# The first two batches by pairs of heads instead of units of 256 tokens, in a retention and low-rank mixer kernel

## The chip, the cores and the metric

The kernel runs on one core of a Trainium2 chip. Five engines work from their own instruction queues: TensorE (PE in the profile, its weight loads PEld), VectorE (DVE), ScalarE (ACT), GpSimd (POOL) and SyncE (SP), which only issues transfers here. The metric is the device time of one execution in microseconds (us); less is better.

## The reference

Eight batches, eight heads, 576 tokens, head dimension 64. A retention layer (attention without softmax, with a decay per head) is followed by a low-rank token mixer and a two-layer channel MLP with a residual.

```python
scores = scale * np.matmul(q, k.transpose(0, 1, 3, 2))
gamma = 1.0 - 2.0 ** (-5.0 - np.arange(H))
Dmat = np.where(rel >= 0, gamma[:, None, None] ** rel[None], 0.0)   # rel = i - j
x = matmul(scores * Dmat, v)            # heads side by side: (8, 576, 512)
u = x + ((x.transpose(0, 2, 1) @ U) @ V).transpose(0, 2, 1)   # rank 32, over tokens
out = u + np.maximum(u @ w_ch1, 0.0) @ w_ch2                  # 512 -> 2048 -> 512
```

The inputs and the output are float32.

## The kernel before

The decay is split: `qscale` and `vscale` hold gamma to the power of plus and minus the position, so scores need only a triangular 0/1 mask. Within a batch the tokens are worked in blocks of 128. A block's output is its own masked scores times v (RV) plus q times a running state k^T v of all earlier blocks (QS); ST adds a block to the state.

A batch has 576 tokens, four and a half blocks, so two batches make nine blocks, and the fifth, index `J`, is shared: its lower 64 rows are batch 0's tail, its upper 64 rows batch 1's head. This is the half chunk (functions with `_J`).

After attention, x (tokens by 512) goes through the mixer: MA computes `a` = U^T x (rank 32 by 512), MH adds V^T a to x and gives u; u^T is needed as the input of the MLP. Y1 is the first layer, one step for each of 16 blocks of 128 hidden columns (`f`): four matmuls of 512 columns into a PSUM buffer of `ps_big` (three buffers), and one ScalarE ReLU copy (L482). Y2 (L511) is the second layer; VectorE adds u (L500) and POOL stores.

The order is written out by hand: each engine works its queue in program order. It has three parts.

- `startup` (L779): SyncE loads q, k, v of batches 0 and 1; batch 0's attention; then u^T of batch 0.
- `first_stretch` (L886): batch 1's attention, in between the Y1 steps of batch 0, which `y(n)` takes from a list; then u^T of batch 1 and the first Y1 steps of batch 1.
- `merge` (L16): the rest. Main work (Y1, Y2) of one pair of batches is mixed with the attention of the next by running cost, and with its loads and casts (`aux_items`). There, chunks of 128 tokens are transposed by the DMA queue (`xbar`, L259), and L275 is their score matmul. The chunks of batch 2 are numbered 9 and on.

In the first two parts, attention works on units of 256 tokens by all eight heads: units 0 and 1 are batch 0, 2 and 3 batch 1. A partition holds two neighbouring tokens, so one loaded piece has runs of 512 bytes. For each unit:

- `load_u` (L566): for each of k, q, v two transfers of 256 KB, four heads each, issued by SyncE.
- `cast_u` (L587): to bf16 on POOL (L592); `scale_u` (L594) multiplies v by its decay.
- `T_u` (L603): 16 TensorE transposes for k or for q into a PSUM tile, then one copy of 1024 columns to SBUF by VectorE (L620) or ScalarE (L618).
- `SC_u` (L626), 16 score matmuls of four heads into PSUM; `mask_u` (L641), one VectorE multiply of 1024 columns; twice a unit.
- `ST_u` (L684) and `Sblk` (L694): the state, copied to `sblk` by ScalarE.
- `RV_u` (L652), `QS_u` (L668), `XS_u` (L676): the output, scaled by VectorE to x.

So x of a batch is complete only after both units, and MA and u^T come after that. For batch 0, u^T is made directly in PSUM: transposing matmuls of x (L859) and then V^T a added on top (L874), copied by ScalarE and VectorE (L882, L884). For batch 1, MH makes u (L421, L427), which is transposed (L448) and copied (L452). `warm(n)` (L185) issues n matmuls without use, 128 by 512, that keep TensorE busy.

POOL also issues the weight transfers: `load_w1` (L194, four pieces) and `load_w2` (L200, eight pieces), which convert to bf16 on the way. SyncE's transfers use eight completion semaphores in turn.

Of the kernel before, what the change touches and what calls it, by code (L numbers as in the profile page):

```python
# [35 lines left out]
def kernel(  # L36
# [23 lines left out]
    J = 4  # L60
# [35 lines left out]
    vscaleU = consts.tile([P, 4, 2, H], FP32, name="vscaleU")  # L96
# [17 lines left out]
    def early_consts():  # L114
# [21 lines left out]
        nc.scalar.activation(out=vscaleU, in_=posU, func=AF.Exp, bias=lnb, scale=-1.0)  # L136
# [29 lines left out]
    def make_u():  # L166
        nc.scalar.activation(out=U_E[:, 0:J, :], in_=U_f[:, 0:J, :], func=AF.Copy)
        nc.scalar.activation(out=U_E[0:HALF, J, :], in_=U_f[0:HALF, J, :], func=AF.Copy)

        ps = ps_s.tile([P, 5, R], FP32, tag="pss", name="pu_o")  # L170
        nc.tensor.matmul(ps, swap, U_E, start=True, stop=True)
        nc.scalar.activation(out=U_O[0:HALF, 1:5, :], in_=ps[0:HALF, 0:4, :], func=AF.Copy)
        nc.scalar.activation(out=U_O[HALF:P, :, :], in_=ps[HALF:P, :, :], func=AF.Copy)
# [59 lines left out]
    def cast_qk(pr, i, rows=slice(0, P), eng=None):  # L233
# [4 lines left out]
        if eng is not None:  # L238
            for j in (1, 0):
                eng.tensor_copy(  # L240
                    out=t[rows, j, :], in_=c["f", j][rows].rearrange("p h d -> p (h d)"))
            return
# [222 lines left out]
    def y1_items(par, by_seg=False):  # L465
        nch = 4 + par
        segs = [(0, 4)] if par == 0 else [(0, 3), (3, 2)]
        items = []

        def Y1(f, seg):  # L470
            if f == 0 and seg == 0:
                st["y1", par] = y1_pool.tile(
                    [P, NF, nch * P], BF16, tag=f"y1{par}", name="y1")
# [86 lines left out]
    un = [dict() for _ in range(4)]  # L560
    st["x", 0] = x_pool.tile([P, NI, dm], BF16, tag="x", name="xt")

    def unit_i0(u):
        return 2 * u + (1 if u >= 2 else 0)

    def load_u(u, which):  # L566
        b = u // 2
        t0 = 2 * P * (u % 2) + HALF * b
        for j in which:
            dram = (q, k, v)[j]  # L570
            for hh in range(2):
                t = stage.tile([P, H, D], FP32, tag="stage", name="stage_t")
                un[u]["f", j, hh] = t
                nc.sync.dma_start(  # L574
                    out=t.rearrange("p (h j) d -> p h (j d)", j=2),
                    in_=dram[b, 4 * hh:4 * hh + 4, t0:t0 + 2 * P, :].rearrange(
                        "h (p j) d -> p h (j d)", j=2),
                )

    def unit_views(u, j, hh):  # L580
        if j not in un[u]:
            un[u][j] = qk_pool.tile([P, 2, dm], BF16, tag="qk", name="qk")
        w = slice(hh * 4 * D, (hh + 1) * 4 * D)
        return (un[u][j][:, :, w].rearrange("p j (h d) -> p h j d", d=D),
                un[u]["f", j, hh].rearrange("p (h j) d -> p h j d", j=2))

    def cast_u(u, j, hh, eng):  # L587
        o, f = unit_views(u, j, hh)
        if eng is nc.scalar:
            nc.scalar.activation(out=o, in_=f, func=AF.Copy)  # L590
        else:
            eng.tensor_copy(out=o, in_=f)  # L592

    def scale_u(u, hh, eng):  # L594
        o, f = unit_views(u, 2, hh)
        eng.tensor_tensor(
            out=o, in0=f,
            in1=vscaleU[:, u, :, 4 * hh:4 * hh + 4].rearrange("p j h -> p h j")[
                :, :, :, None].to_broadcast([P, 4, 2, D]),
# [3 lines left out]
    def T_u(u, j, eng):  # L603
        pst = ps_big.tile([P, 2 * NHP, P], BF16, tag="big", name="pst")
        for jj in range(2):
            for hp in range(NHP):
                nc.tensor.transpose(
                    pst[:, jj * NHP + hp, :], un[u][j][:, jj, hp * P:(hp + 1) * P], ident)
        t = qkT_pool.tile([P, 2 * NHP, P], BF16, tag="qkT", name="qkT")
        un[u]["T", j] = t  # L610
        o, i_ = t, pst
        if j == 0:

            o = t.rearrange("p a b -> p (a b)").rearrange(
                "p (hp t j) -> p j hp t", hp=NHP, j=2)
            i_ = pst.rearrange("p (j hp) t -> p j hp t", j=2)
        if eng is nc.scalar:
            nc.scalar.activation(out=o, in_=i_, func=AF.Copy)  # L618
        else:
            eng.tensor_copy(out=o, in_=i_)  # L620

    def qT(u):
        return un[u]["T", 0].rearrange("p a b -> p (a b)").rearrange(
            "p (hp t) -> p hp t", hp=NHP)

    def SC_u(u, hh, pool_, tag):  # L626
        psc = pool_.tile([P, 2, NHP, P], FP32, tag=tag, name="psc")
        kT, qt = un[u]["T", 1], qT(u)
        for hp in range(2):
            for jj in range(2):  # L630
                for s in range(2):
                    for hl in range(2):
                        r = slice(hl * HALF, (hl + 1) * HALF)
                        m = slice(s * HALF, (s + 1) * HALF)
                        nc.tensor.matmul(  # L635
                            psc[m, hl, hp * 2 + jj, :], kT[r, jj * NHP + 2 * hh + hp, m],
                            qt[r, 2 * hh + hp, s * P:(s + 1) * P], start=True, stop=True,
                        )
        un[u]["psc", hh] = psc

    def mask_u(u, hh):  # L641
        ret = ret_pool.tile([P, H, P], BF16, tag="ret", name="ret")
        nc.vector.tensor_tensor(  # L643
            out=ret.rearrange("p (a j) i -> p a (j i)", j=2),
            in0=un[u]["psc", hh].rearrange("p a b i -> p (a b i)").rearrange(
                "p (a ji) -> p a ji", a=4),
# [3 lines left out]
        un[u]["ret", hh] = ret  # L650

    def RV_u(u, hh):  # L652
        if "po" not in un[u]:
            un[u]["po"] = ps_o.tile([P, 2, dm], FP32, tag="po", name="po")
        for hp in range(2):
            for hl in range(2):
                h = 4 * hh + 2 * hp + hl
                for jj in range(2):
                    for s in range(2):
                        r = slice(s * HALF, (s + 1) * HALF)  # L660
                        nc.tensor.matmul(  # L661
                            un[u]["po"][:, s, h * D:(h + 1) * D],
                            un[u]["ret", hh][r, hl * 4 + hp * 2 + jj, :],
                            un[u][2][r, jj, h * D:(h + 1) * D],
                            start=(h == 0 and jj == 0), stop=True, skip_group_check=True,
                        )

    def QS_u(u, s, slot):  # L668
        for hp in range(NHP):
            nc.tensor.matmul(  # L670
                un[u]["po"][:, s, hp * P:(hp + 1) * P],
                qT(u)[:, hp, s * P:(s + 1) * P], sblk[:, slot, hp, :],
                start=False, stop=True, skip_group_check=True,
            )

    def XS_u(u, c0=0, c1=2):  # L676
        i0, n = unit_i0(u) + c0, c1 - c0
        nc.vector.tensor_tensor(  # L678
            out=st["x", 0][:, i0:i0 + n, :].rearrange("p s (h d) -> p s h d", d=D),
            in0=un[u]["po"][:, c0:c1, :].rearrange("p s (h d) -> p s h d", d=D),  # L680
            in1=qscale[:, i0:i0 + n, :, None].to_broadcast([P, n, H, D]), op=ALU.mult,
        )

    def ST_u(u, rows, acc, start):  # L684
        for hp in range(NHP):
            for jj in range(2):
                nc.tensor.matmul(  # L687
                    acc[:, hp, :], un[u][1][rows, jj, hp * P:(hp + 1) * P],
                    un[u][2][rows, jj, hp * P:(hp + 1) * P],
                    start=(start and hp == 0 and jj == 0), stop=True,  # L690
                    skip_group_check=True,
                )

    def Sblk(acc, slot):  # L694
        for hl in range(2):
            r = slice(hl * HALF, (hl + 1) * HALF)
            nc.scalar.activation(
                out=sblk[r, slot, :, hl * D:(hl + 1) * D],
                in_=acc[r, :, hl * D:(hl + 1) * D], func=AF.Copy)

    LO, HI, ALL = slice(0, HALF), slice(HALF, P), slice(0, P)

    def T_J(r):
        c = ch[0, J]
        pst = ps_big.tile([P, 2 * NHP, P], BF16, tag="big", name="pst")
        for j in range(2):
            for hp in range(NHP):
                nc.tensor.transpose(
                    pst[:, j * NHP + hp, r], c["qk"][r, j, hp * P:(hp + 1) * P],
                    ident[r, r])  # L710
        if "qkT" not in c:
            c["qkT"] = qkT_pool.tile([P, 2 * NHP, P], BF16, tag="qkT", name="qkT")
        nc.scalar.activation(out=c["qkT"][:, :, r], in_=pst[:, :, r], func=AF.Copy)

    def SC_J(r):
        c = ch[0, J]
        c["psc"] = ps_sc.tile([P, 2, NHP, P], FP32, tag="psc", name="psc")
        for hp in range(NHP):
            for hl in range(2):
                d = slice(hl * HALF, (hl + 1) * HALF)  # L720
                nc.tensor.matmul(
                    c["psc"][r, hl, hp, r], c["qkT"][d, NHP + hp, r], c["qkT"][d, hp, r],
# [3 lines left out]
    def mask_J(r):  # L726
        c = ch[0, J]
        if "ret" not in c:
            c["ret"] = ret_pool.tile([P, H, P], BF16, tag="ret", name="ret")
        nc.vector.tensor_tensor(  # L730
            out=c["ret"].rearrange("p (hp hl) i -> p hl hp i", hl=2)[r, :, :, r],
            in0=c["psc"][r, :, :, r],
            in1=tri[r, None, None, r].to_broadcast([HALF, 2, NHP, HALF]), op=ALU.mult,
        )

    def RV_J(r):
        c = ch[0, J]
# [276 lines left out]
```

## Time and profile before

| what | value |
|---|---|
| median of 3 runs | 337.58 us (336.85 to 338.22) |
| span of the profiled execution | 335.6 us |
| PE busy | 320.9 us, 96% |
| ACT, DVE, POOL busy | 139.2, 138.0, 78.2 us |
| chain that ended last, PE's share | 91% |
| of it Y1 (L477) and Y2 (L511) | 38% and 36% |
| Y1 step of 512 columns, one matmul | 0.33 us mean (with its end modelled) |
| POOL cast 128x512 (L592) | 0.61 us |
| mask 128x1024 (L643) | 1.22 us |
| k^T or q^T copy of 1024 columns | 0.69 us on VectorE (L620), 1.25 us on ScalarE (L618) |
| transfers | 36.85 MB read, 9.44 MB written |

The span runs from the first to the last instruction of the program; the device time has a little around it. "Chain" is the work that ended last, followed back step by step to whatever released it. Idle time of an engine off that chain costs nothing. In the views by stretch, each engine's busy time stands with its number of instructions, then the clock that TensorE was granted (1.00 is full), the busy share of the transfer engines and what they moved.

### The profile page before, as it was taken

What the parts mean: (1) busy time and instruction counts of PE and PEld (TensorE: products, weight loads), DVE (VectorE), ACT (ScalarE), POOL (GpSimd) and SP (SyncE); (2) the same over time, 40 slices, a digit from 0 to 9 for tenths busy, and PEclk for the clock granted to TensorE, in tenths of its full rate; (3) what the DMA queues carried; (4) which work ended last, traced back from release to release, by engine and by line L of the source; (5) the groups of instructions that cost most, each with busy time, mean ns of one, the idle gap of its engine ahead of it and who ended that gap; (6) DMA issues with size and microseconds to landing.
All of it is one profiled execution on the core that took longest, in us unless ns stands there. A gap on an engine that the chain in (4) does not pass through costs nothing.

```text
span 335.6 us, 6997 instructions
## 1 busy us (share of the span) xinstructions
PE 320.9 (96%) x2926; PEld 179.9 (54%) x2948; DVE 138.0 (41%) x190; ACT 139.2 (41%) x290; POOL 78.2 (23%) x112
## 2 busy tenths in 40 slices
PE   6688999899999999999999999999999999999996
PEld 3375554576544445446764455457754455457644
DVE  5453346433564234534356244524365144510022
ACT  2543665776210077107850176017740264037400
POOL 5686741211231140114102220222111100110000
PEclk9955999999999999999999999999999999999999
DMA  7999999999999929994998959995933400340012
GB/s 212 239 228 266 237 217 182 187 179 223 213 249 234 234 73 192 207 198 105 198 177 190 213 123 168 195 241 71 200 76 99 142 2 1 79 126 2 0 64 94
DMA packets 151311, 53.17 MB, mean 158 GB/s; under 512 B 131984, under 2 KB 148752, under 8 KB 151280
## 3 DMA queue, kind: packets, MB, share of 16 engines
q1 hardware_dynamic: 144512, 40.40, 64.7%
q0 software_dynamic: 6768, 12.32, 14.6%
q8 instruction: 23, 0.38, 0.5%
q14 instruction: 8, 0.07, 0.1%
HBM read 36.85 MB, written 9.44 MB: 138 GB/s over the span
## 4 chain that ended last, share of the span: by engine, by line
PE 91%; SPq 2%; issue 2%; DVE 2%; DMA 1%; ACT 1%; POOL 0%
PE ps_y L477 38%; PE ps_y L511 36%; PE psc L275 3%; PE po L314 2%; PE pss L687 2%; PE pss L340 2%; DMA stage_t<-in_q_dram 1%; SPq L574 1%; PE ph L421 1%; PE ps_y L522 1%; PE pa L394 1%; PE po L300 1%; PE po L661 1%; PE xT L859 1%; DVE xt L678 1%
## 5 line engine op out<-in xcount | busy, mean ns | idle before, releaser
L477 PE MATMUL ps_y<-uT,w_sb 128*128 128x256 bf16 (+2 forms) x768 | 137.0, 328 | 1.5 <-ACT uT L452 1.4
L482 ACT ACTIVATE y<-ps_y 128x384 bf16<-128x384 f32 (+2 forms) x192 | 90.0, 489 | 114.9 <-PE ps_y L477 114.2
L511 PE MATMUL ps_y<-w_sb,y 128*128 128x512 bf16 x538 | 124.3, 379 | 1.6 <-issue 0.8
L477 PEld LDWEIGHTS <-w_sb 128*128 128x128 bf16 x768 | 71.6, 98 | 46.7 <-issue 3.1
L511 PEld LDWEIGHTS <-y 128*128 128x128 bf16 x560 | 52.4, 98 | 60.3
L500 DVE TENSOR_TENSOR o_sb<-ps_y,u 128x512 f32<-128x512 f32 (+2 forms) x38 | 25.2, 663 | 76.6 <-PE ps_y L511 74.4
L503 POOL DMA_DIRECT2D out_dram<-o_sb x31 | 17.3, 558 | 158.6 <-DVE o_sb L500 152.8
L285 DVE TENSOR_TENSOR ret<-psc,tri 128x1024 bf16<-128x1024 f32 x24 | 29.4, 1225 | 47.3 <-PE psc L275 47.3
L254 POOL TENSOR_TENSOR vt<-stage_t,vscale 128x512 bf16<-128x512 f32 (+1 forms) x29 | 30.0, 1047 | 50.6 <-DMA stage_t<-in_v_dram 50.1
L325 DVE TENSOR_TENSOR xt<-po,qscale 128x512 bf16<-128x512 f32 x27 | 18.6, 691 | 25.9 <-PE po L314 25.9
L427 DVE TENSOR_TENSOR u<-ph,xt 128x768 bf16<-128x768 f32 (+2 forms) x24 | 21.8, 951 | 13.5 <-PE ph L421 13.5
L348 ACT ACTIVATE s_sb<-pss 128x512 bf16<-128x512 f32 x24 | 14.3, 597 | 8.3 <-PE pss L340 7.3
L245 ACT ACTIVATE qk<-stage_t 128x512 bf16<-128x512 f32 x27 | 16.5, 622 | 2.1 <-DVE o_sb L500 2.1
L243 DVE CAST qk<-stage_t 128x512 bf16<-128x512 f32 x27 | 16.3, 604 | 0.0
L400 ACT ACTIVATE a_sb<-pa 128x128 bf16<-128x128 f32 x8 | 2.2, 276 | 33.0 <-PE pa L394 33.0
L643 DVE TENSOR_TENSOR ret<-psc,triU 128x1024 bf16<-128x1024 f32 x8 | 9.7, 1222 | 11.3 <-PE psc L635 11.3
L314 PEld LDWEIGHTS <-ret 128*128 128x128 bf16 x216 | 10.0, 98 | 4.2
L592 POOL CAST qk<-stage_t 128x512 bf16<-128x512 f32 x16 | 9.6, 611 | 7.0 <-DMA stage_t<-in_q_dram 5.3
L275 PEld LDWEIGHTS <-qkT 64*128 64x128 bf16 x216 | 6.1, 94 | 9.1 <-issue 8.7
L275 PE MATMUL psc<-qkT 64*128 64x128 bf16 x216 | 10.7, 219 | 0.0
L314 PE MATMUL po<-vt,ret 128*128 128x64 bf16 x216 | 10.7, 193 | 0.0
L340 PE MATMUL pss<-vt,qk 128*128 128x128 bf16 (+1 forms) x96 | 9.3, 219 | 0.0
(103 smaller groups left out, 165.5 us busy)
## 6 DMA issues: line engine op xcount, KB each, us to landing
stage_t<-in_k_dram SPq DMA_DIRECT2D x32, 256.0 KB, 4.1
stage_t<-in_q_dram SPq DMA_DIRECT2D x32, 256.0 KB, 4.9
stage_t<-in_v_dram SPq DMA_DIRECT2D x32, 256.0 KB, 5.5
out_dram<-o_sb POOLq DMA_DIRECT2D x31, 256.0 KB, 3.8
w_sb<-in_moe_w_ch_dram POOLq DMA_DIRECT2D x4, 512.0 KB, 8.4
w_sb<-in_moe_w_ch_dram POOLq DMA_DIRECT2D x8, 256.0 KB, 10.2
stage_t<-in_k_dram SPq DMA_DIRECT2D x8, 128.0 KB, 4.2
stage_t<-in_q_dram SPq DMA_DIRECT2D x8, 128.0 KB, 4.0
```

The source lines that it names most:

```text
L245: nc.scalar.activation(out=t[rows, 0, :], in_=c["f", 0][rows].rearrange("p h d -> p (h d)"), func=AF.Copy)
L254: (eng or nc.gpsimd).tensor_tensor(out=c["v"][rows], in0=c["f", 2][rows], in1=vscale[rows, i, :, None].to_broadcast([n, H, D]), op=ALU.mult,)
L275: nc.tensor.matmul(psc[:, hl, hp, :], qkT[r, NHP + hp, :], qkT[r, hp, :], start=True, stop=True,)
L285: nc.vector.tensor_tensor(out=ret.rearrange("p (hp hl) i -> p hl hp i", hl=2), in0=c["psc"], in1=m[:, None, None, :].to_broadcast([P, 2, N ...
L314: nc.tensor.matmul(c["po"][:, hl, hp * D:(hp + 1) * D], c["ret"][:, h, :], c["v"][:, h, :], start=(first and hp == 0), stop=True, skip_gro ...
L325: nc.vector.tensor_tensor(out=xt[:, i, :].rearrange("p (hp hl d) -> p hl hp d", hl=2, d=D), in0=c["po"][:, :, 0:NHP * D].rearrange("p hl ( ...
L427: nc.vector.tensor_tensor(out=st["u", par][:, i0 - base:i0 - base + n, w].rearrange("p s (c d) -> p c s d", c=2), in0=ph[k][:, :, 0:n, :], ...
L477: nc.tensor.matmul(ps[:, 0:n, :], w1_sb[:, cc, f * P:(f + 1) * P], st["uT", par][:, c0:c0 + n, cc, :], start=(cc == 0), stop=(cc == NCC - 1),)
L482: nc.scalar.activation(out=st["y1", par][:, f, c0 * P:(c0 + n) * P], in_=ps[:, 0:n, :].rearrange("p s t -> p (s t)"), func=AF.Relu)
L500: nc.vector.tensor_tensor(out=o_sb[:, 0:n], in0=ps[:, 0:n], in1=st["u", par][:, c, w], op=ALU.add)
L503: (nc.sync if last else nc.gpsimd).dma_start(out=out_flat[r0:r0 + P, w], in_=o_sb[:, 0:n])
L511: nc.tensor.matmul(ps, st["y1", par][:, f, c * P:(c + 1) * P], w2_sb[:, f, :], start=(f == 0), stop=(f == NF - 1),)
```

## The change

Attention of batches 0 and 1 is worked by pairs of heads instead of units of tokens. One pair (`hp`, 0 to 3) covers all 512 tokens of a batch's four full blocks (for batch 0 the first 512, for batch 1 the last 512), and its two heads' 128 columns of x. MA and u^T need x by columns, so each pair can go from load to its own part of u^T.

- Loads: `load_h` issues, for each pair and each of k, q, v, two transfers of 128 KB (runs of 512 bytes as before). All of them, the half chunk's too, are in SyncE's queue, in the order in which they are used: pair 0, half chunk of batch 0, V, U, pairs 1 to 3, half chunk of batch 1, pairs 0 to 3 of batch 1. The constants are emitted after the loads.
- Half chunks: the two 64-row pieces are worked separately, both in the lower rows. Batch 0's outputs go to free columns of the pair's own PSUM tile (`RJ_h`, columns 256 to 383), scaled by `XSJ_h`.
- Each pair: `Tk_h`, `Tq_h` (four transposes each, into two parts of one PSUM tile), `SC_h`, `mask_h`, `ST_h`, `RQ_h` (RV and QS), `XS_h`, `XT_h` (transposing matmuls of x), `MA_h` (its 32 rows of a), `UT_h` (V^T a added, copies to u^T).
- Batch 1's u^T is made in the same way, the shared block by `UT_J`; `MH` of both batches moves behind the first Y1 steps of batch 1, and the transposes of u (L448) go.
- `make_u` is split; `dummy` matmuls like those of `warm` are put into the tiles that are about to be written.
- w1's pieces are issued by POOL between casts: piece 0 after pair 2, piece 1 in the half chunk of batch 1, pieces 2 and 3 in pairs 0 and 1 of batch 1.
- Six Y1 steps of batch 1, not three, are done before `merge`; the loads and casts of chunks 9 to 12 are emitted together before them.

```diff
-    def load_u(u, which):
-        b = u // 2
-        t0 = 2 * P * (u % 2) + HALF * b
...
+    def load_h(b, hp, j, eng):
+        t0 = HALF * b
+        t = stage.tile([P, H, D], FP32, tag="stage", name="stage_t")
+        sl[b][hp]["f", j] = t
+        for u in range(2):
+            eng.dma_start(
+                out=t.rearrange("p (u h j) d -> p u h (j d)", u=2, h=2)[:, u],
+                in_=(q, k, v)[j][
+                    b, 2 * hp:2 * hp + 2, t0 + 2 * u * P:t0 + 2 * (u + 1) * P, :].rearrange(
                         "h (p j) d -> p h (j d)", j=2),
...
+    def dummy(ap, n):
+        for _ in range(n):
+            nc.tensor.matmul(
+                ap, ident, ident[:, None, :].to_broadcast([P, 4, P]), start=True, stop=True,
+                skip_group_check=True)
+
+    def Tk_h(b, hp, ek):
+        c = sl[b][hp]
+        c["pst"] = ps_big.tile([P, 2 * NHP, P], BF16, tag="big", name="pst")
+        t = qkT_pool.tile([P, 2 * NHP, P], BF16, tag="qkT", name="qkT")
+        c["kT"], c["qT"] = t[:, 0:4, :], t[:, 4:8, :].rearrange("p a b -> p (a b)")
+        for u in range(2):
+            for jj in range(2):
+                nc.tensor.transpose(c["pst"][:, 2 * u + jj, :], c["qk"][:, 1, jj, u, :], ident)
+        copy(ek, c["kT"], c["pst"][:, 0:4, :])
...
+    def ST_h(b, hp, engs, n=0):
+        c = sl[b][hp]
+        acc_t = ps_s.tile([P, 4, P], FP32, tag="pss", name="acc")
+        dummy(acc_t, n)
...
+        def add(hl, n0, n1, lhsT, rhs):
+            nc.tensor.matmul(
+                acc[hl * HALF:(hl + 1) * HALF, n0:n1, :], lhsT,
+                rhs[:, None, :].to_broadcast([rhs.shape[0], n1 - n0, D]),
+                start=new[hl], stop=True, skip_group_check=True)
...
+    def startup():
...
+        def pool_h(hp):
+            cast_h(0, hp, 1, nc.gpsimd)
+            cast_h(0, hp, 0, nc.gpsimd)
+            scale_h(0, hp, nc.gpsimd)
+
+        A, V, G = nc.scalar, nc.vector, nc.gpsimd
+        warm(10)
+        pool_h(0)
+        cast_J(0, G)
+        scale_J(0, G)
+        pool_h(1)
+        pool_h(2)
+        load_w1(0)
...
+        SC_h(0, 2, 2)
+        mask_h(0, 2)
+        ST_h(0, 2, (A, A))
+        cast_h(0, 3, 1, A)
+        XT_h(0, 1)
+        MA_h(0, 1, A)
+        Tk_h(0, 3, V)
+        cast_h(0, 3, 0, V)
+        UT_h(0, 1, (A,))
+        Tq_h(0, 3, A)
+        scale_h(0, 3, G)
+        RQ_h(0, 2)
+        RJ_h(2)
+        XS_h(0, 2)
+        XSJ_h(2)
+        SC_h(0, 3, 2)
+        mask_h(0, 3)
+        ST_h(0, 3, (A, A))
+        XT_h(0, 2)
+        MA_h(0, 2, A)
+        UT_h(0, 2, (A,))
+        RQ_h(0, 3)
+        RJ_h(3)
+        XS_h(0, 3)
+        XSJ_h(3)
+        XT_h(0, 3)
+        warm(3)
+        MA_h(0, 3, A)
+        UT_h(0, 3, (A, V))
...
     def first_stretch():
...
+        for hp in range(NHP):
+            cast_h(1, hp, 1, G)
+            cast_h(1, hp, 0, G)
+            if hp < 2:
+                load_w1(hp + 2)
+            scale_h(1, hp, G)
+            T_h(1, hp, V, A)
+            if hp:
+                XT_h(1, hp - 1)
+                MA_h(1, hp - 1, V)
+            else:
+                RV_J(1, 0, H)
+                XS_J(1, 0, H)
             y(1)
+            SC_h(1, hp)
+            mask_h(1, hp)
+            ST_h(1, hp, (A, A))
+            y(1)
+            if hp:
+                UT_h(1, hp - 1, (V,))
+            y(1)
+            RQ_h(1, hp)
+            XS_h(1, hp)
         for f in range(0, NF, 2):
             load_w2(f)
+        XT_h(1, 3)
         y(1)
+        MA_h(1, 3, A)
+        UT_J(0, A)
         y(16)
+        UT_h(1, 3, (A, V))
+        UT_J(2, A)
+        aux = aux_items(NI, NI + 4)
+        for fn in aux:
             fn()
         Y1, rest = y1_items(1, by_seg=True)
...
+        for seg in (1, 0):
+            for f in range(2):
+                Y1(f, seg)
         MH0(outs0[0])
+        for fn in rest[2:4]:
+            fn[1]()
+        MH1(outs1[0])
+        for fn in rest[4:6]:
+            fn[1]()
+        MH1(outs1[1])
+        return rest[6:]
```

## The prediction

> **What bounds the kernel now.** I read the strips first, then the chain of waits in order of time, then stretches with the granted clock, then single groups in the first 66 us.
>
> ```profile
> PE   6688999899999999999999999999999999999996
> PEld 3375554576544445446764455457754455457644
> ...
> PEclk9955999999999999999999999999999999999999
> DMA  7999999999999929994998959995933400340012
> ```
>
> Each digit is a fortieth of the span, 8.4 us. TensorE is full from about 60 us to the end, so a change in the first two batches is worth what it moves TensorE's place in its own queue, no more. The clock strip has its only low digits at the start, and the DMA strip is full there too.
>
> ```profile
> 30.92 0.59 ACT uT L882
> ...
> 32.14 1.82 PE ps_y L477 x4
> ...
> 45.26 0.58 DVE xt L678
> 45.84 0.56 issue
> 46.40 0.69 DVE qkT L620
> 47.09 0.04 issue
> 47.13 1.02 PE ps_y L477 x4
> ...
> 61.18 1.46 PE ps_y L477 x8
> ...
> 64.20 3.64 PE ps_y L477 x28
> 67.84 0.33 PE psc L275 x8
> ```
>
> These are start, length and work along the chain. Batch 0's u^T is ready at 31.5 and its first Y1 begins at 32.1; batch 1's Y1 begins at 61.2; the first score matmul of batch 2 (L275) starts at 67.8, with five of batch 1's sixteen Y1 steps done. I compare the kernels at that last point. The three middle lines matter later: after RV, TensorE stood 1.9 us because VectorE did x first (L678) and only then the copy of the next k^T (L620).
>
> ```profile
> 7.60:11.00 3.40, 2.19 (x48) 1.51 (x48) 0.78 (x1) 1.55 (x2) 2.03 (x4) 1.00 1.14 254
> 11.00:14.40 3.40, 1.66 (x20) 0.76 (x12) 1.58 (x2) 2.09 (x2) 1.68 (x3) 1.00 1.21 225
> 14.40:17.80 3.40, 2.55 (x56) 1.64 (x57) 2.39 (x2) 1.87 (x4) 3.17 (x5) 1.00 1.32 223
> 17.80:21.20 3.40, 2.88 (x42) 2.49 (x43) 2.19 (x3) 1.51 (x4) 3.35 (x4) 0.50 1.13 173
> ...
> 31.50:34.90 3.40, 3.34 (x22) 1.42 (x22) 1.28 (x3) 1.69 (x4) 3.31 (x6) 0.50 1.20 243
> 34.90:38.30 3.40, 3.40 (x31) 1.97 (x30) 0.84 (x2) 2.33 (x5) 1.20 (x3) 1.00 1.22 268
> ```
>
> Busy us of PE, PEld, DVE, ACT and POOL, then the granted clock. Three stretches with TensorE busy 6.4 of 10.2 us, and the clock halves; it comes back after the first stretch of Y1 (2.8 us from 32.1).
>
> **The change, part by part.** I work out S, when batch 0's u^T is complete, then A, when batch 1's Y1 begins, then the first L275.
>
> *Loads.* 256 KB loads become twice as many of 128 KB. SyncE issues one per 0.54 us (0.74, 1.24, 1.78, 2.33 in the chain), the first landed 3.0 us after issue (first cast 3.77). 24 pieces and the 6 loads of half chunk, V and U: 0.74 + 30 x 0.54 + 3 = 19.9 for the last of batch 0. The bounds for the 24 extra issues are 0 (hidden behind the compute chain) and 24 x 0.54 = 13 us. I take 0: the third and fourth pairs' transposes come at 15.6 and 20.2 by the ledger below, and that pair's k and q are in by 18. If that cover goes, each late us is a us on S. A page rule bears on this: the Trainium skill, "DMA: Bandwidth & Descriptors", section "Rules for kernel authors", asks to coalesce many small transfers. No run here shows 128 KB pieces at the start; by its wish the loads would cost something, by the issue rows nothing.
>
> *Batch 0's chain.* Durations from the first 66 us: mask 1.22 (128x1024), POOL cast 0.61, scale 1.06, sblk copy 0.38, a_sb 0.27, q^T copy half of L618's 1.25 = 0.65, k^T copy half of L620's 0.69 plus start = 0.42, x in two halves 0.85 (L678: 1.22 for 1024; L755: 0.68 for 512), half chunk's x 0.3, uT 0.6. TensorE: 8 transposes 0.45 less their overlap = two of 0.25, SC 0.35, ST 0.5, RV+QS+half chunk 0.75, a dummy 0.22. The built program adds one wait the diff hides: the q transposes write the same PSUM tile as the k transposes and wait for VectorE's copy of k^T. In order: pair 0 casts to 5.8, k^T copy after the constants at 6.2, SC 7.5, mask 8.8, sblk 9.1, RQ 9.8; half chunk and V until 12; pair 1 SC 14.6, mask 15.8, RQ 17.3; pair 2 SC 18.1, mask 19.7, sblk 19.5. Pair 3's k cast is on ScalarE behind that (20.1), its q cast on VectorE (21.3), its q transposes 21.6, and pair 2's RQ stands behind them on TensorE: 22.4. Then x 23.25, half chunk 23.55, mask 24.8, RQ 25.9, x 27.05, XT, three dummies and MA 28.0, a_sb 28.3, UT 28.6, copies **S = 29.0**. Before: 31.5 to 32.1.
>
> *Batch 1 between Y1 of batch 0.* TensorE work from before's full-clock rows: a lone Y1 step 0.97 (32 to 61 us), 16 of them 15.5. Per pair: transposes 0.45, XT 4 x 0.069 = 0.28, MA 0.30, SC 0.35, ST 0.5, UT 0.22, RV 16 x 0.0215 and QS 4 x 0.069 = 0.62; together 2.72, four times 10.9. ST has no row (64-column weights, both halves of the output): 0.40 if the halves run side by side as SC's do, 0.65 if not; I take the middle. Half chunk: 0.35 + 0.35 + 0.37 + 0.1, and UT_J 12 x 0.056, 1.85. Sum 28.2. Before did this in 29.1 with 1.4 us lost to the half clock.
>
> *New waits there.* In each pair VectorE has x (0.85) and then the k^T copy (0.42) before the q transposes may go, while TensorE has only the k transposes (0.25): 1.05 idle, four times 4.2. Queued behind are XT, MA and a Y1 step. This is the 45.26 pattern, now once a pair. The half chunk's SC waits 0.35; the last XT waits for x 0.9; MA's copy stands behind a Y1 eviction, 0.65; the last copies 0.1. Sum 6.2, so **A = 29.0 + 28.2 + 6.2 = 63.4**, against 61.2.
>
> *After it.* The casts of chunks 9 and 10 now stand on ScalarE before Y1's evictions: 0.45 beyond three PSUM buffers. Chunk 10's q was cast at 61.0 before (0.62, not waiting), so it has landed. Before L275 there are now eight Y1 steps instead of five, 8 x 1.08 = 8.64, and the u of both batches (ph: 0.34 + 0.34 + 0.23 = 0.91), and 0.46 as between these pieces before: 73.9. Three Y1 steps less follow (3.24): 70.65 against 67.84, **2.8 us late with a full clock**. POOL's w1 and w2 issues are the same twelve at 0.74 to 0.84; w1's first piece goes at 17 and needs some 8 us, before S; nothing on the path. The memset, constants and allocations moved in the source cost nothing: their engines have them in the same place. The transposes by the DMA queue for chunk 9 were issued at 60.4 and have slack of 3 us before; A later gives them more.
>
> *Clock.* Changes lie 3.4 us apart in multiples (4.2, 17.8, 34.9). By my ledger TensorE has about 2.3, 2.9 and 2.9 us in the stretches up to 17.8 (23 dummies instead of 11, most of them early), then 1.9, 2.5 and 2.2 up to 28.1: 6.6 of 10.2, as before its loss. So I put the loss at 28.1, the regain at 34.9 as before: 0.5 on the tail of the chain, and 5.4 us of Y1 at half, 2.7: 3.2. Bounds: 0 (kept), and 4.65 (lost at 21.2: S 32.45 and 1.2 more). The Trainium skill, "TensorE: Matmul & The Clock Gate", section "Why this matters for your kernels", warns only of idle gaps over some 3 us; my ledger has none over 1.1, so by it the clock stays and the sum is the 2.8 alone. The trace lost it at 17.8 without such a gap (busy 2.55 of 3.4), and I follow the trace.
>
> The span is 335.6 and about 2 us lie around it, 337.6, which is the median of the runs shown (337.58). 337.6 + 2.8 + 3.2 = **343.6**.
>
> **Rivals.** *Clock kept*: 340.4. For it: more dummies; against: few after 18 us. *Pairs paced by their loads* (the other side): the hand-overs overlap better than my serial ledger, and S follows the last load of batch 0 at 19.9 by one chain (scale 1.06, ST 0.5, sblk 0.8, RQ 0.75, x 1.15, MA and UT 1.3) at 25.5; with UT pipelined 25. Price -4.0 with the clock kept: 336.4. It decides from S + idle below 32.4, where A falls under 61.2 in worth. For it: TensorE is busy only some 60% in my ledger; against: VectorE's x, copy, mask are in series there. Batch 1's waits halved as well would give 334.3; the casts before the evictions then hold Y1 at chunk 10's arrival (cast 61.0 before), so little below that. *Loads the bound*: each 128 KB as slow as a 256 KB step (0.95 us between casts) brings batch 0 in by 3.8 + 29 x 0.95 = 31, S 37: 350. Against: the DMA rate in the strip is already full. *It doesn't do what it says*: u^T of batch 0 no earlier than 32; that is the early loss of clock, 345.
>
> **How the numbers follow.** A clock loss, 343.6 to 345: 0.43. Clock kept, 340.4: 0.17. Loads: 0.03. These are the slower ones, 0.63. Load-paced: 0.37, of which 0.17 ends within 0.5% (1.7 us, about what a measurement of this kernel can tell) and 0.20 faster. The range reaches from 336.0, which leaves the faster ones out, to 347; the slower cases alone have 339 to 347.
>
> **What would show it.** S right: uT's copies of batch 0 end near 29. Waits right: VectorE's k^T copies in batch 1 follow x directly, and TensorE idles 1 us before the q transposes of each pair. Clock right: 0.50 in stretches between 28 and 35. Wrong: Y1 begins near 25, or TensorE is full from 25 to 60. First L275 near 74 to 77 is my sum; below 71 the change is a gain.

## The result and the profile after

The changed kernel takes 348.87 us (median of 4 runs, 346.52 to 350.8) against 337.29 us (336.85 to 338.22) for the kernel before: a ratio of 1.032, with a 95% interval from 1.027 to 1.037. It is slower, as forecast, by 11.6 us instead of 6.0, and above the range. The profiled execution took 350.8 us, with a span of 349.0, the longest of the four.

The page's strips of the changed kernel, a fortieth of the span (8.7 us) for each digit:

```profile
PE   8878888899999999999999999999999999999996
PEld 3444354456644444545775445446764445457644
...
PEclk9895599999999999999999999999999999999999
DMA  6799989739999996999499888896874400070012
```

TensorE looks busier in the first slices than before (8878 against 6688), and yet everything is later: 23 dummy products instead of 11 (beside the first ten of both) count as busy, and so does the longer time of products at half clock (three dummies 1.29 us instead of 0.65). A busy digit at the start is no progress. From the ninth slice on the PE strip is the same as before.

The chain of waits of the changed kernel in order of time (start, length, work), at the places that were shown of the kernel before:

```profile
36.68 0.60 PE xT L864
37.28 1.82 PE ps_y L483 x4
...
48.13 0.76 DVE xt L726 x2
48.88 0.34 DVE qkT L589
...
49.27 0.38 PE pst L632 x4
...
74.19 1.14 ACT qk L250 x2
75.33 0.28 ACT y L488
...
75.66 0.81 PE ps_y L483 x4
...
84.43 0.33 PE psc L280 x8
```

Batch 0's first Y1 begins at 37.3 (32.1 before; the forecast had u^T at 29.0), batch 1's at 73.9 (61.2), batch 2's first score product at 84.4 (67.8). With the three Y1 steps that are already done there, 84.43 - 3.24 - 67.84 = 13.35 us late. The spans differ by 349.0 - 335.6 = 13.4, so all of it is lost before 84 us: 5.1 in the start, 7.5 in the stretch from there to batch 1's Y1 (36.6 instead of 29.1), 0.7 after it. The middle lines are the forecast's wait: VectorE's x, then the copy of k^T, and TensorE idle until the q transposes.

The start of the changed kernel, in the same chain:

```profile
22.18 0.38 ACT sblk L587
...
22.58 0.64 ACT qk L587
...
23.27 0.41 PE pst L625 x4
...
24.05 0.79 DVE qk L589
...
24.88 0.40 PE pst L632 x4
25.27 0.54 PE po L710 x16
...
29.93 0.70 PE pa L843 x5
```

ScalarE copies pair 2's state (sblk), then casts pair 3's k; TensorE waits for it with the k transposes, then VectorE casts pair 3's q, and pair 2's RQ stands behind all this on TensorE until 25.3 (forecast: 21.6). It isn't the loads: pair 3's k landed at 18.44 and its q at 19.34, the last of batch 0 at 20.46 (forecast 19.9).

Stretches of the changed kernel, laid along the changes of clock (busy us of PE, PEld, DVE, ACT, POOL, then granted clock, share of the transfer engines, GB/s):

```profile
18.37:21.79 3.42, 2.90 (x65) 1.91 (x63) 1.79 (x5) 1.37 (x4) 2.44 (x4) 1.00 0.80 166
21.79:25.20 3.41, 1.75 (x18) 1.00 (x16) 1.88 (x3) 2.24 (x5) 1.68 (x3) 1.00 1.14 193
25.20:28.61 3.41, 3.41 (x54) 2.04 (x54) 1.23 (x4) 0.74 (x1) 1.14 (x2) 0.50 1.20 282
...
38.86:42.27 3.41, 3.41 (x26) 1.57 (x25) 0.28 (x1) 2.24 (x5) 2.27 (x3) 0.50 1.17 243
```

The stretch in which TensorE waits for those casts has 1.75 us of work in 3.41, and at its end the clock halves. It comes back at 42.3, after a stretch filled mostly by Y1: 17.1 us at half clock, most of them on the chain. An earlier drop, from 11.5 to 15.0 us, adds 3.4.

### The profile page after: what moved, and what is told of

It is laid out like the page before. It is cut to its first block, busy times and chain, and to the rows that moved or that the text cites. A ratio compares the mean times of both kernels' runs of the same rounds, so it can differ in the third digit from the quotient of the medians.

```text
span 349.0 us, 7266 instructions
## 1 busy us (share of the span) xinstructions
PE 335.4 (96%) x3024; PEld 182.3 (52%) x3024; DVE 142.5 (41%) x216; ACT 140.6 (40%) x302; POOL 77.9 (22%) x111
## 4 chain that ended last, share of the span: by engine, by line
PE 93%; DVE 2%; ACT 1%; DMA 1%; SPq 1%; issue 1%; POOL 0%; ACTq 0%
PE ps_y L483 37%; PE ps_y L517 35%; PE psc L280 3%; PE po L319 2%; PE pss L345 2%; PE ph L426 1%; DMA stage_t<-in_q_dram 1%; PE acc L677 1%; PE ps_y L528 1%; PE pa L843 1%; PE pw L195 1%; PE po L305 1%; DVE xt L726 1%; PE xT L864 1%; PE po L710 1%; SPq L578 1%
## 5 line engine op out<-in xcount | busy, mean ns | idle before, releaser
L517 PE MATMUL ps_y<-w_sb,y 128*128 128x512 bf16 x560 | 126.9, 380 | 0.0
L506 DVE TENSOR_TENSOR o_sb<-ps_y,u 128x512 f32<-128x512 f32 (+2 forms) x38 | 25.2, 663 | 73.2 <-PE ps_y L517 71.0
L290 DVE TENSOR_TENSOR ret<-psc,tri 128x1024 bf16<-128x1024 f32 x24 | 29.4, 1224 | 45.2 <-PE psc L280 45.2
L259 POOL TENSOR_TENSOR vt<-stage_t,vscale 128x512 bf16<-128x512 f32 x27 | 28.1, 1050 | 53.5 <-DMA stage_t<-in_v_dram 41.6
L432 DVE TENSOR_TENSOR u<-ph,xt 128x1024 bf16<-128x1024 f32 (+2 forms) x24 | 21.8, 952 | 13.6 <-PE ph L426 13.6
L589 POOL CAST qk<-stage_t 128x512 bf16<-128x512 f32 (+1 forms) x18 | 11.0, 610 | 13.0 <-DMA stage_t<-in_k_dram 8.1
L726 DVE TENSOR_TENSOR xt<-po,qscale 128x256 bf16<-128x256 f32 x16 | 6.1, 420 | 12.7 <-PE po L823 6.9
```

The costliest lines, as they stand in the source:

```text
L259: (eng or nc.gpsimd).tensor_tensor(out=c["v"][rows], in0=c["f", 2][rows], in1=vscale[rows, i, :, None].to_broadcast([n, H, D]), op=ALU.mult,)
L290: nc.vector.tensor_tensor(out=ret.rearrange("p (hp hl) i -> p hl hp i", hl=2), in0=c["psc"], in1=m[:, None, None, :].to_broadcast([P, 2, N ...
L432: nc.vector.tensor_tensor(out=st["u", par][:, i0 - base:i0 - base + n, w].rearrange("p s (c d) -> p c s d", c=2), in0=ph[k][:, :, 0:n, :], ...
L506: nc.vector.tensor_tensor(out=o_sb[:, 0:n], in0=ps[:, 0:n], in1=st["u", par][:, c, w], op=ALU.add)
L517: nc.tensor.matmul(ps, st["y1", par][:, f, c * P:(c + 1) * P], w2_sb[:, f, :], start=(f == 0), stop=(f == NF - 1),)
```

## The experiments

Theory: three terms add up. The start is late by its own chain (pair 3's casts, and the one PSUM buffer of `ps_s`); its idle time costs the clock; batch 1's pairs cost some 6 us in the stretch, half of it the wait for k^T. Rivals: one of the two batches is all of it; the clock falls whatever is done; the loads pace it. Every kernel's numbers stand here: when the record of batch 0's first Y1 product starts and how long it is from there to batch 1's, both from the profiled execution; the time; and the mean granted clock of its runs (0.01 is some 7 us at half clock).

| kernel | first Y1, us | to batch 1's Y1, us | median, us (range) | clock of the runs |
|---|---|---|---|---|
| before | 32.07 | 29.1 | 337.29 (336.85 to 338.22) | 0.974 (profiled) |
| changed | 37.21 | 36.6 | 348.87 (346.52 to 350.80) | 0.971, 0.975, 0.990, 0.989 |
| units_pairs | 27.97 | 35.1 | 341.19 (337.64 to 342.34) | 0.990, 0.985, 0.985, 1.000 |
| pairs_units | 36.72 | 32.0 | 344.39 (342.57 to 347.27) | 0.960, 0.975, 0.984, 0.975 |
| k_first | 36.70 | 36.1 | 349.71 (349.32 to 350.30) | 0.975, 0.971, 0.975, 0.975 |
| cast3_pool | 32.54 | 36.2 | 345.04 (344.01 to 346.25) | 0.990, 0.994, 1.000, 0.989 |
| c3_no_dummies | 34.02 | 35.9 | 347.38 (346.90 to 350.19) | 0.959, 0.951, 0.960, 0.960 |
| c3_pa_big | 30.25 | 35.3 | 342.72 (342.02 to 344.34) | 1.000, 1.000, 0.999, 1.000 |
| own_q_y | 36.27 | 33.4 | 343.64 (343.00 to 346.67) | 0.975, 0.989, 0.989, 0.985 |
| before_late_half | 25.84 | 30.0 | 336.31 (335.46 to 339.46) | 0.970 to 0.995 |
| filled | 32.16 | 35.3 | 345.22 (344.45 to 347.60) | 1.000, 1.000, 1.000, 0.985 |
| pa_big | 35.60 | 36.6 | 346.20 (345.08 to 349.20) | 0.975, 0.989, 0.984, 0.989 |
| c3_pa_own | 30.27 | 32.1 | 341.05 (339.61 to 344.44) | 0.999, 1.000, 0.995, 0.995 |
| units_own | 27.34 | 31.8 | 336.39 (334.66 to 339.00) | 0.990 to 1.000 |

The kernel before, run beside them, had medians of 336.87 (the first four), 335.92 (the next four) and 336.20 (the last four).

### Which batch: units_pairs and pairs_units

```diff
 units_pairs: startup() of the kernel before (half chunk's upper part and w1's second piece left
 to the stretch), then first_stretch() of the changed one
+        load_J(1, nc.sync)
+        for hp in range(NHP):
+            for j in (1, 0, 2):
+                load_h(1, hp, j, nc.sync)
 pairs_units: startup() of the changed kernel, then first_stretch() of the one before
+        load(0, J, (1, 0, 2), seg=1)
+        load_u(2, (1, 0, 2))
+        load_u(3, (1, 0, 2))
```

> Batch 0 as in the kernel before (units), batch 1 by pairs as in the changed one. Theory (the loss has two parts that add: batch 0's u^T is 5.2 us late, 37.3 against 32.1 us, and the stretch from there to batch 1's Y1 is 36.6 instead of 29.1 us): u^T back at 32, stretch about 35.5 (a little less of it at half clock), so batch 1's Y1 at 67.6 and some 342 to 343.5 us in all. Rival (the start is all of it, the stretch only long because it starts late and at half clock): first Y1 at 32, the stretch back near 30, 337 to 338.5 us.

> Batch 0 by pairs as in the changed kernel, batch 1 by units as before. Theory (two parts that add): u^T of batch 0 stays at 37 us, the stretch is 29 to 31 us, 342 to 344 us. Rival (the start is hidden, batch 1's stretch is all): 337 to 339 us. Rival (the half clock from 25 us is all): first Y1 at 37 and 344 us or more, with the clock low till 42.

Both halves cost. Batch 1 by pairs keeps its long stretch (35.1) even when it starts 9 us earlier; batch 0 by pairs keeps its late u^T (36.7) with batch 1 by units. The ratios to the kernel before are 1.014 (1.006 to 1.021) and 1.026 (1.019 to 1.033). So it is not one batch alone. The rival of the clock isn't excluded here: the signs that it named for pairs_units (first Y1 at 37, 344 us or more, a low clock until 42) all came, with a clock that was low until 41.7; filled, below, answers it. units_pairs was a little faster than the theory's sum: its first Y1 came at 28 instead of 32, with 6.8 us at half clock instead of 17.1. That the clock is the reason is not shown (before_late_half, below).

### The wait for k^T: k_first and own_q_y

```diff
 k_first: the next pair's k transposes and copy ahead of x; a Y1 step ahead of XT
             RQ_h(1, hp)
+            if hp + 1 < NHP:
+                head(hp + 1)
             XS_h(1, hp)
 own_q_y: q transposes in their own tiles; the same Y1 step ahead of XT
+            pq = ps_big.tile([P, 2 * NHP, P], BF16, tag="big", name="psq")
+            t = qkT_pool.tile([P, 2 * NHP, P], BF16, tag="qkT", name="qqT")
             T_h(1, hp, V, A)
+            y(1)
             if hp:
                 XT_h(1, hp - 1)
                 MA_h(1, hp - 1, V)
...
-            y(1)
             SC_h(1, hp)
```

> In batch 1 each pair's k transposes and the copy of k^T now stand before the previous pair's x on VectorE, and a Y1 step lies between the q transposes and the XT that needs x. Theory (TensorE's 1.15 us idle in three pairs is the wait for that copy behind x): 0.7 to 0.8 us less per pair, 2 to 2.5 us less in all, 346 to 347 us. Rival (the wait only moves to XT, which now waits for x): 0 to 0.5 us less, 348.5 us.

> Changed kernel; in batch 1 the q transposes get their own PSUM and SBUF tiles, so that they no longer wait for VectorE's copy of k^T, and a Y1 step stands between them and the XT that needs x. Theory (each pair's 1.15 us of TensorE idle is that wait): 0.9 to 1.1 us less per pair in three pairs, 0.4 in the first, batch 1's Y1 3 us earlier after the first Y1, 345.5 to 346 us. Rival (the stretch is bound elsewhere, by VectorE or by GpSimd's casts): less than 1 us, 348 us or more.

k_first moved the wait instead of removing it: TensorE still stood 0.5 us between the k and q transposes, and ST, with MA now shortly ahead of it, took 0.65 us in the chain instead of 0.46. A pair's period went from 6.87 to 6.54, and the time at the same clock (0.971 to 0.975) from 349.7 and 350.8 to between 349.3 and 350.3: nothing that can be told. own_q_y removes the shared tile. The chain of own_q_y:

```profile
46.89 0.22 PE pst L625 x4
47.12 0.22 PE psq L637 x4
47.34 0.86 PE ps_y L483 x4
48.20 0.25 PE xT L859 x4
```

k transposes, q transposes and Y1 now follow one another with no VectorE row between them, and a pair's period is 5.90: 0.97 less, what the theory said. The stretch is 3.2 us shorter. At a clock near 0.99 it takes 343.0 to 343.95 against 346.5 and 348.0, at 0.975 346.7 against 349.7: 3 us or somewhat more. The median lies 2 us below the expectation, with three of its four runs at the higher clock.

### Pair 3's casts, the PSUM buffer: cast3_pool, pa_big, c3_pa_big

```diff
 cast3_pool
         load_w1(0)
+        pool_h(3)
...
-        cast_h(0, 3, 1, A)
...
-        cast_h(0, 3, 0, V)
...
-        scale_h(0, 3, G)
 pa_big (and, on top of cast3_pool, c3_pa_big)
-        pa = ps_s.tile([P, P], FP32, tag="pss", name="pa")
+        pool_, tag = (ps_s, "pss") if b else (ps_big, "big")
+        pa = pool_.tile([P, P], FP32, tag=tag, name="pa")
```

> The casts and the scaling of batch 0's fourth pair go to GpSimd behind w1's first piece; ScalarE and VectorE lose theirs. Theory (pair 3's q transposes at 24.9 us, behind VectorE's cast, hold pair 2's RQ): pair 2's RQ starts near 23 instead of 25.3, first Y1 at 35 to 35.8 instead of 37.3, 1.5 to 2.3 us less, 347 us. Rival (another wait, such as the one PSUM buffer that MA, ST and the dummies share, ends at the same time): first Y1 within 0.5 us of 37.3, no change.

> Changed kernel; batch 0's MA in a PSUM buffer of the pool of three, and nothing else. Theory (this wait is a term by itself): MA01 no longer waits for the state's copies, but pair 3's k cast on ScalarE, behind those copies, still holds the k transposes until 23.2, so 0.3 to 1 us less at equal clock, 347 to 348.5 us. Rival (it and the casts add in full): first Y1 2 us earlier, 346 to 347 us.

> On top of cast3_pool: batch 0's MA writes a PSUM buffer of the pool of three instead of the single one that the state sums use too. Theory (MA01 and MA02 wait for both sblk copies, 0.85 us each, with k transposes, RQ and SC of the next pair queued behind): 1.2 to 1.8 us less, first Y1 at 31, 343.5 us. Rival (the k transposes then wait for a buffer of the three, or for the casts): within 0.5 us of cast3_pool.

cast3_pool brings the first Y1 4.7 us forward, twice what was expected, and most of that goes with the clock. In the changed kernel the first drop had already put pair 1's SC at 16.72; here it starts at 15.53. Of the 2.2 us by which pair 2's RQ starts earlier (23.1 against 25.3) that leaves 1.0 for the casts; the other 2.5 come later, where the clock now is full until 29.4. pa_big alone starts its first Y1 at 35.6 with the clock at half from 23.4 to 40.4, and its time is 2.7 us lower in the median, but 0.5 (349.2 against 349.7) and 1.1 to 1.4 (345.1 and 345.4 against 346.5) at like clocks, 0.975 and 0.989: nearer to the theory, though the clock's scatter is as large. On top of cast3_pool it gives 2.3 us at the first Y1, 30.25, and the clock stays full in all four runs. Pair 3's RQ, ahead of cast3_pool's drop at 29.4, starts at 26.44 instead of 27.46: 1.0 is the buffer, and the other 1.3 come where cast3_pool runs at half clock.

### The clock: c3_no_dummies and filled

```diff
 c3_no_dummies: cast3_pool without its dummy products after the first ten
-        warm(2)
...
-        SC_h(0, 1, 3)
+        SC_h(0, 1)
...
 filled: the changed kernel with eight more, in a tile of ps_big
+        fill(3)
         MA_h(0, 1, A)
+        fill(2)
         Tk_h(0, 3, V)
...
+        fill(3)
         MA_h(0, 2, A)
```

> On top of cast3_pool (first Y1 at 32.5 us, 345.0 us): the dummy products after the first ten are all left out (46 weight loads and products, 23 of each). Theory (the dummies stand on the chain: 4.8 us of them in its rows from 11.8 us on, some 2 us of which other waits would fill): first Y1 at 29.5 to 31, 342 to 343.5 us. Rival (without them the clock is lost earlier and for longer): first Y1 at 33 or later, half clock before 20 us, 346 us or more.

> Changed kernel with eight more dummy products where TensorE waits in batch 0's second half: three ahead of MA01 (it waits 0.85 us for the state's copies), two ahead of pair 3's k transposes (waiting for the cast on ScalarE, 0.6 us), three ahead of MA02. At full clock each takes 0.22 us, so all lie inside those waits. Theory (the clock falls at 25 us because TensorE was too idle before; the late half clock is 6 to 7 of the 11.6 us): clock kept to the first Y1, first Y1 near 33 to 34, 344 to 346 us. Rival (the clock falls whatever TensorE does there, or the dummies only lengthen the chain): first Y1 at 37 to 38, 348 to 350 us.

Without dummies the rival was right: the clock halves at 9.8 us, after a stretch of 3.4 us in which TensorE was busy for 1.69, and stays so for 27.3 us; 347.38 against 345.04. With eight more of them, nothing else changed, the clock is full in three of four runs and the first Y1 starts at 32.2 instead of 37.2. Stretches of filled, laid as those of the changed kernel:

```profile
18.91:22.32 3.41, 3.41 (x53) 1.95 (x53) 2.13 (x4) 1.66 (x4) 1.78 (x3) 1.00 0.87 133
22.32:25.73 3.41, 2.88 (x60) 1.64 (x57) 1.68 (x6) 1.34 (x2) 0.00 (x0) 1.00 1.20 221
25.73:29.15 3.42, 3.06 (x47) 1.79 (x43) 1.21 (x2) 1.62 (x4) 2.85 (x4) 1.00 1.09 244
```

The same casts, the same loads and the same waits, but 2.88 us busy where the changed kernel had 1.75, and no drop. So filled is the changed kernel at full clock, and splits its loss: the clock is 350.8 - 344.45 = 6.35 us in the profiled executions, and 348.87 - 345.22 = 3.65 in the medians, since two runs of the changed kernel had a clock of 0.99 without any filling; the rest is not the clock. Nor is all of the 6.35 the work of the eight products. The first of them comes at 20.6, and the drop at 11.5 is missing in filled as well, with the same queue of TensorE up to there: its stretch before that place lies from 8.67 to 12.08 and holds 2.77 us of work, the changed kernel's from 8.13 to 11.54 holds 2.48.

### Sums and a faster version: c3_pa_own, before_late_half, units_own

```diff
 c3_pa_own: cast3_pool, pa_big and own_q_y together
 units_own: units_pairs and own_q_y together
 before_late_half: the kernel before, with
-        load_w1(1)
-        cast_qk(0, J, HI, nc.gpsimd)
-        scale_v(0, J, HI, nc.gpsimd)
 moved from startup() to the head of first_stretch(), and
+        y(1)
         T_J(HI)
```

> The three edits together: pair 3's casts on GpSimd, batch 0's MA in a buffer of its own, batch 1's q transposes in their own tiles with a Y1 step ahead of XT. Theory (the parts add: first Y1 at 30.3, 33.4 us to batch 1's Y1, first score product of batch 2 near 74 against 81.2 less the three Y1 steps of before): 339 to 340.5 us. Rival (what comes early there is given back, because batch 2's u^T by the DMA transpose is late, as in before_late_half and c3_pa_big): 341.5 to 343 us.

> Kernel before; only the upper half chunk's casts and scaling and the second piece of w1 on GpSimd are moved from the start to behind batch 0, as units_pairs has them, with a Y1 step ahead of the half chunk's transposes. Theory (units_pairs' first Y1 at 28 instead of 32 is its shorter time at half clock, not this move): 336 to 338 us, no change. Rival (the move frees the start): first Y1 at 28 to 29.5, 333.5 to 335 us.

> Batch 0 by units as before, batch 1 by pairs with the q transposes' own tiles and the Y1 step ahead of XT (units_pairs and own_q_y together). Theory (parts add: 341.2 less 3 to 4): 337 to 338.5 us, no faster than before. Rival (the loads or batch 2's DMA transposes then set the end): 340 us or more. If batch 1 by pairs is worth anything by itself, this would show it: below 335 us.

The three edits add up in the trace (30.27, then 32.1, batch 2's first score product at 72.88), and the profiled execution took 339.61; the median of 341.05 lies between the two expectations, with runs from 339.6 to 344.4 at nearly the same clock, so the rival isn't excluded. In the trace of c3_pa_own nothing is given back: batch 2's u^T landed at 118.3, and TensorE needed it at 118.6. units_own is as fast as the kernel before, ratio 1.001 (0.997 to 1.005), not faster. before_late_half, too: 1.001 (0.998 to 1.004), although its first Y1 is 6.2 us earlier and the first score product of batch 2 3.2 us. The chain of before_late_half shows where 2 us of that went:

```profile
107.34 8.17 DMA uT<-u
...
115.56 1.90 PE ps_y L477 x8
```

Batch 2's u^T is made by a DMA transpose. The kernel before issued it at 107.0 and had it 5.9 us later, ahead of need; here it was issued at 107.3 and took 8.2, and TensorE waited 2.0 us. It could not follow the earlier u: VectorE had u ready at 107.0 before and at 103.8 here, but SyncE was still issuing the transposes of a chunk (L262) until 107.2. Of the 3.2 us gained at the start, 2 are given back there. Whether the move itself made the start shorter or the clock, full until 52.9 here and halved at 17.8 before, the run doesn't tell. No version of these beats the kernel before.

## Why the prediction was right or wrong

**Right: direction and comparison point.** The loss at the first score product of batch 2 is the loss of the span within 0.1 us.

**Right: the loads at nothing.** Issues come 0.51 us apart, and the last of batch 0 landed 0.6 us later than forecast; pair 3's q was in at 19.3 instead of by 18, still 4.7 before its cast. The rival "loads the bound" named S 37 and 350 us, close to what came, but that is luck, by another cause: with the loads unchanged filled has 32.2 and c3_pa_big 30.3.

**Right: the new waits of batch 1, and what comes after it.** Before the q transposes of each pair TensorE idled 0.96 us by its records (forecast 1.05), behind x and the copy of k^T as forecast, and own_q_y got 0.97 back. The stretch took 35.3 at full clock (34.4), the part after it 10.6 (10.5).

**Wrong: S = 29.0.** This is the step that failed, the ledger "In order" of batch 0's chain. At full clock (filled) the first Y1 starts at 32.2, 3.2 us late (the last copy of u^T even ends at 33.1). Pair 1's SC ended at 15.8 instead of 14.6: TensorE had hardly a gap from 11.3 on, and 1.7 us of that are eight dummies (0.215 each) that the ledger doesn't list. Pair 2's SC ended at 20.0 instead of 18.1, the q cast at 23.4 instead of 21.3. And the ledger missed a wait: MA, the state's sums and the dummies share one PSUM buffer. PE's timeline in filled:

```profile
27.04 0.45 PE L847 MATMUL pa<-xt,U_E 128*32 128x128 bf16 x5
27.85 0.38 PE L868 MATMUL xT<-V,a_sb 32*128 32x512 bf16 x1 [0.36 <-ACT a_sb L587]
28.17 0.41 PE L714 MATMUL po<-vt,ret 64*128 64x64 bf16 x16
```

MA of pair 2 could start only when ScalarE had copied the state out, and pair 3's RQ, whose mask was done at 26.9, waited behind it and UT until 28.2. RQ ended at 29.2, where the ledger had 25.9. Casts and buffer together are 1.9 of the 3.2 us (32.2 to 30.25, both at full clock); the last 1.3 were not taken apart.

**Wrong: how the clock is lost.** I asked for three thin stretches in a row and put the loss at 28.1; one thin stretch was enough, at 25.2, with another drop at 11.5 in the profiled execution. And I let it fall on 5.4 us of Y1, where it fell on the chain of batch 0 as well. The size, 3.2, is 6.35 in the profiled execution; that the medians give 3.65 is luck, since the runs differ in how often the clock fell (0.971 to 0.990).

The sum with the clock kept closes: 340.4 + 3.2 (S) + 0.9 (stretch) = 344.5, against 344.45 in the trace of filled and 345.22 in its median. So of the 5.3 us by which the median exceeds 343.6, 4.1 are these two terms.

**The rivals.** Clock kept, 340.4: filled is that case, and takes 344.45, since S and the stretch were forecast too short. Paced by their loads, 336.4: no; the last load of batch 0 landed at 20.5 in the changed kernel, and the first Y1 of the fastest start by pairs, c3_pa_big, is at 30.3, not at 25. Doesn't do what it says, 345 with u^T not before 32: the nearest in kind, with too small a price; its early loss of clock was one part of the cause.

## What to carry to other kernels

In a start of small, dependent steps write down the queue of each engine and the owner of each buffer, not only the durations along the path: here a shared PSUM buffer cost 1.0 us, and 1.7 us of dummy products that the ledger doesn't list stood ahead of pair 1's scores. Price the clock by the thinnest single stretch of 3.4 us of the new order, fill that one, and test before fillers are left out; one run's clock is not the next one's. And before a start is made faster, look for what later does not move with it, as SyncE's queue ahead of batch 2's transfer.

## What the runs showed of the hardware

- In all traces the clock changes at multiples of 3.41 us from one another. Cut into such stretches, from the start to 56 us, all 13 drops follow a stretch in which TensorE's products were on record for 44 to 75% of the time, and none a fuller one. That isn't sufficient: other stretches of 49 to 74% were followed by none. What else decides is open.
- The clock came back only after a stretch at half clock that was 97% busy or more, and not after each of these: not at 28.6 in the changed kernel, after 3.41 busy of 3.41 in which most products had 64 rows, but at 42.3 after Y1's. Whether the rows decide wasn't tested.
- The Trainium skill, "TensorE: Matmul & The Clock Gate", section "What's actually happening", has the clock drop after at least one idle window of some 3.4 us. The window agrees (3.41 here); the idleness doesn't: at 25.2 it fell after a window with 1.75 us of work, and the measurement decides.
- VectorE's cast of pair 3's q, 128x512, took 0.78 us in the changed kernel, 0.73 in k_first and 0.46 in own_q_y, each time beside a cast or the issue of a weight transfer on POOL, and 0.42 in filled and pa_big, where POOL stood idle. No run varied that alone, so the cause is open.
